# Narrowing weights with ScalarE's sign, two wider products in den_i and a shorter product of ones

## The chip, the cores and the metric

The kernel runs on one core of a Trainium2 chip. The metric is device time in microseconds, from launch to end, as the median of several runs. A core has five engines that run side by side and wait for each other through semaphores: TensorE (PE in the profile; PEld is its loading of weights), VectorE (DVE), ScalarE (ACT), GpSimd (POOL) and SyncE (SP), whose queue issues most of the DMAs.

## The reference

Two blocks follow each other. The first is a linear attention with sketched features, over 4 batches, 4 heads and 1088 positions of 32 numbers:

```python
def phi(x):
    a = np.einsum('rd,bhsd->bhsr', S1, x)
    b = np.einsum('rd,bhsd->bhsr', S2, x)
    return np.einsum('bhsi,bhsj->bhsij', a, b).reshape(*x.shape[:-1], r * r)   # r = 8
q_p, k_p = (phi(q), phi(k))
kv = np.einsum('bhsf,bhsd->bhfd', k_p, v)
z = np.sum(k_p, axis=2)
num = np.einsum('bhsf,bhfd->bhsd', q_p, kv)
den = np.einsum('bhsf,bhf->bhs', q_p, z)[..., None] + 1e-06
attn = (num / den).astype(np.float32)
```

The second takes the result as x with 4352 rows and 128 columns, and is a gated feed-forward layer with 1536 inner columns:

```python
gate = 1.0 / (1.0 + np.exp(-(x @ w_gate)))
val = x @ w_val
out = (gate * val @ w_out).astype(np.float32)
```

S1, S2 and the three weight matrices are given in double precision, q, k and v in single precision. The kernel reads the doubles as pairs of 32-bit words and makes single-precision numbers of them on the chip. This is what "narrowing" means below.

## The kernel before

**Tiling.** The inner dimension of the layer is cut into NJ = 12 blocks of 128, and the tokens into eight chunks of 512 and a last one of 256. A *wave* is one block of one chunk: two products give gate and value (`wave`, L501), ACT makes the sigmoid (`sg`, L509), DVE multiplies (`g`, L540), and a further product adds into the output (`moeout`, L382, in the first chunk; `prod`, L338, in most of the others, which use a scheme with fewer products whose sums POOL forms at L324 and L328). A list `todo` holds the output products back by some waves. Between the waves, `slot` places the steps of the attention of the next batch at wave numbers that are written out by hand.

**Engines' order.** The order of the instructions on PE, DVE, ACT and POOL is the order of the program. SP's order is left to the scheduler.

**The head.** Before the first wave can start, the first half of batch 0 goes through the whole attention: S1 and S2 are narrowed and turned (`st`, L1103), then k is turned (L599), multiplied with S (`kps`, L630), turned back (`kab`, L640), its outer products are formed (`kp`, L709), and from these come `kvz` (L836), its copy `kvd` (L871), the transposed `nd` (L905, L922), the numerators `nps` (L1039) and at last `xT` (L1060), numerators times reciprocals of the denominators. `warm` issues products of ones that nobody reads. One of 256 columns stands right after `st` (L1111), ahead of `kps`; others stand at L1149 and L1171. `den_i` (L989) belongs to the batches 1 to 3: it sums the denominators over the index i, in four products of 32 columns, one for each head, each into its own 32 partitions.

**Narrowing, old form** (`narrow`, L83). A double's high word carries sign, exponent and the upper part of the mantissa; its low word gives three more bits. Six instructions follow each other for each part:

- POOL caps the high word between -122880 and 122880 (`cap`, L97), and ACT makes an integer of the top of the low word (`tail`, L101);
- DVE shifts the capped word left by three and masks it (L105), and puts the sign bit back (L109, `head`);
- ACT squares the capped word (L117), which serves to set small values to zero, and POOL adds `tail` to `head` (L118);
- DVE multiplies `head` by 0 or 1, as the square is under or over a bound, and writes `w_sb` (L127).

The weights are narrowed in parts: part 0 is block 0 of w_gate and w_val, part 1 is block 1 of these, part 2 is blocks 0 and 1 of w_out (`narrow_01`, three parts of 256 columns), and block 2 of all three (`narrow_w(2)`, 384 columns) is the fourth. The first two parts are needed by the first two waves, the third by the first `moeout`, the fourth by the third wave. The blocks 3 to 11 are narrowed in `w1`, between the waves of the first chunk, and are not changed.

Of the kernel before, what the change touches and what calls it, by code (L numbers as in the profile page):

```python
# [20 lines left out]
def kernel(  # L21
# [12 lines left out]
    nc = tc.nc  # L34

    B, H, S, D = q.shape
# [4 lines left out]
    NJ = DFF // P  # L41
# [38 lines left out]
    wide = S1.dtype == I64  # L80
    assert all((a.dtype == I64) == wide for a in (S2, moe_w_gate, moe_w_val, moe_w_out))

    def narrow(out, bits, eng, bank=None, copies=None):  # L83

        p, n, m = bits.shape[:3]
        lo, hi = bits[:, :, :, 0].bitcast(U32), bits[:, :, :, 1]

        def tmp(dt, tag, bufs):
            return sbN.tile([P, 3, P], dt, tag=tag, name=tag, bufs=bufs)[:p, :n, :m]

        cap, tail = tmp(I32, "cap", 6), tmp(I32, "tail", 5)
        eng.tensor_scalar(  # L97
            out=cap.bitcast(F32), in0=hi.bitcast(F32), scalar1=122880.0, scalar2=-122880.0,
            op0=ALU.min, op1=ALU.max,
        )  # L100
        nc.scalar.activation(out=tail, in_=lo, func=ACTF.Copy, scale=2.0**-29)  # L101
        yield

        head = tmp(I32, "head", 3)
        nc.vector.tensor_scalar(  # L105
            out=head, in0=cap, scalar1=3, scalar2=0x3FFFFFF8,
            op0=ALU.logical_shift_left, op1=ALU.bitwise_and,
        )
        nc.vector.scalar_tensor_tensor(  # L109
            out=head, in0=cap, scalar=-0x40000000, in1=head, op0=ALU.bitwise_and, op1=ALU.bitwise_or  # L110
        )
        yield
        square = cap.bitcast(F32)
        if bank:
            square = pso.tile([P, 512], F32, tag=bank, name="square")[:, : n * m]
            square = square.rearrange("p (n m) -> p n m", n=n)
        nc.scalar.activation(out=square, in_=cap.bitcast(F32), func=ACTF.Square)  # L117
        nc.gpsimd.tensor_tensor(out=head, in0=head, in1=tail, op=ALU.add)  # L118
        yield

        head = head.bitcast(F32)
        if copies:
            square, head = (
                bass.AP(tensor=x.tensor, offset=x.offset, ap=[list(x.ap[0]), [0, copies], [1, m]])
                for x in (square, head)
            )
        nc.vector.scalar_tensor_tensor(  # L127
            out=out, in0=square, scalar=1.265625 * 2.0**-30, in1=head, op0=ALU.is_ge, op1=MUL
        )
        yield  # L130


    s4 = const.tile([2 * R, 4, D], F32, tag="s4", name="s4")
# [14 lines left out]
    w_in = {}  # L148
# [40 lines left out]
    def narrow_01(part, step):  # L189
        if wide:  # L190
            if step == 0:
                i = (slice(0, 2), part) if part < 2 else (2, slice(0, 2))
                narrowing["01", part] = narrow(
                    w_sb[:, i[0], i[1]],
                    w_in[0][:, i[0], i[1]],
                    nc.gpsimd,
                    "acc0" if part else "acc1",
                )
            next(narrowing["01", part])


    def load_rows(src, b, t, parts=((0, T, nc.sync),)):
        for t0, t1, eng in parts:
# [95 lines left out]
    )  # L299
    eps = const.tile([P, 1], F32, tag="eps")  # L300
    nc.gpsimd.memset(eps, 1e-6)
    zb = const.tile([P, H, 32], F32, tag="zb", name="zb")
    nc.gpsimd.memset(zb, 0.0)
    nc.gpsimd.memset(v_sb[64:, :, 0], 0.0)
# [181 lines left out]
    def w1():  # L486

        ci = moe["ci"]
        t0, tw = tok_chk[ci]
        jn = TCH // tw  # L490
        j0 = moe["w"] * jn
        wv = psm.tile([P, 2, TCH], F32, tag="wave", name="wave")

        tp = tw // 2 if ci == 0 and j0 == 0 else tw
        turn = (moe["w"] // 2) % 2
        for o in range(0, tw, tp):
            for which in range(2):
                for jj in range(jn):
                    for c in (0,) if ci == 0 else (1 - turn, turn):
                        d = slice(0, P) if ci == 0 else slice(64 * c, 64 * c + 64)  # L500
                        nc.tensor.matmul(  # L501
                            out=wv[d, which, jj * tw + o : jj * tw + o + tp],
                            lhsT=w_sb[:, which, j0 + jj, d],
                            rhs=xT[:, t0 + o : t0 + o + tp],
                            start=True,
                            stop=True,
                        )
        sg = sbG.tile([P, TCH], F32, tag="sg", name="sg")
        nc.scalar.activation(out=sg, in_=wv[:, 0], func=ACTF.Sigmoid)  # L509
        if ci == 0:  # L510
            if j0 == 1:
                narrow_01(2, 3)
            if 0 < j0 < NJ - 2:
                narrow_w(j0 + 1, 3)
            narrow_w(j0 + 2, 1)
            narrow_w(j0 + 2, 2)
            if j0 < 3:
                narrow_w(j0 + 3, 0)
            if j0 > 1:
                narrow_w(j0 + 4, 0)  # L520
            if j0 == NJ - 3:
                weight_sums(0, NJ // 4)
        if ci == 1 and j0 == 1:
            weight_sums(NJ // 4, NJ // 2)
        if moe["w"] % 2 == 0:
            moe["g"] = sbG.tile([P, 2, TCH], F32, tag="g", name="g")
        pair, odd, n = moe["g"], moe["w"] % 2, moe["n"]

        def glu():
            g = pair[:, odd]  # L530
            todo = moe["todo"]
            if jn == 2:
                nc.vector.tensor_tensor(  # L533
                    out=g.rearrange("p (j u s y) -> p j y u s", j=2, u=2, y=4),
                    in0=wv[:, 1].rearrange("p (j y u s) -> p j y u s", j=2, u=2, y=4),
                    in1=sg.rearrange("p (j y u s) -> p j y u s", j=2, u=2, y=4),
                    op=MUL,
                )
            else:
                nc.vector.tensor_tensor(out=g, in0=wv[:, 1], in1=sg, op=MUL)  # L540
            if not fast(ci):
                lag = 4 if ci else 2
                part = (ci, j0, jn, g.rearrange("p (j t) -> p j t", j=jn))
# [443 lines left out]


    def den_i(b, dps):  # L989
        for h in range(H):  # L990
            nc.tensor.matmul(
                out=dps[32 * h : 32 * h + 32],
                lhsT=mask["head"][:, h % 2, :],
                rhs=PD[b][:, h // 2, :],
                start=True,
                stop=True,
            )
        return dps
# [109 lines left out]
        start=True,  # L1108
        stop=True,
    )  # L1110
    warm(256)  # L1111
    st_ = st_[:, : 2 * R].rearrange("p (n r) -> p n r", n=2)
    sk = const.tile([P, 2, 2, R], F32, tag="sk")
    nc.vector.tensor_tensor(
# [28 lines left out]
    mult10 = ab(None, (0, 1, 0), (psm, "wave"))  # L1143
    for pi in range(2):
        outer(0, pi, NJK - 1, NJK, eng=nc.gpsimd)
    for part in range(2):
        narrow_01(part, 0)
    spread_z()
    warm(512)  # L1149
    for pi in range(2):  # L1150
# [6 lines left out]
    def rest(turn, rc, dT):  # L1157
        kv0([1, 2, 3, 4, 0])
        for pi in range(2):
            outer(0, pi, 5, NJK - 1)  # L1160
        kv0(range(5, NJK))
        turn()
        nt = rc.shape[1] - 1
        nc.scalar.activation(out=rc[:, :nt], in_=dT[:, :nt, :2], func=ACTF.Identity, bias=eps)
        kvd(0)
        narrow_01(0, 1)
        narrow_01(0, 2)
        ndt(0)

    divide = dn(0, 0, rest)  # L1170
    warm(256)  # L1171

    def head1():
        narrow_01(1, 1)
        narrow_01(0, 3)
        narrow_01(1, 2)
        narrow_01(2, 0)
        narrow_w(2, 0)

    divide((0, 4), (4, 8), between=head1)  # L1180
    narrow_01(1, 3)
    narrow_01(2, 1)
    narrow_01(2, 2)

    slot(None, 1)
    cq = {}
# [172 lines left out]
```

## Time and profile before

| What | us |
|---|---|
| median of three runs (lowest, highest) | 293.69 (293.63, 294.33) |
| the profiled execution, its own time | 294.1 |
| span of the profiled execution, first to last instruction | 292.3 |
| PE busy | 286.5 |
| DVE busy | 188.8 |
| POOL busy | 162.7 |
| ACT busy | 92.1 |
| first wave starts | 15.28 |
| first moeout starts | 19.33 |

In a line of a timeline the numbers are start and duration in microseconds; then come the engine, the line of the kernel, the operation, what it writes and reads, the shapes, and how many instructions are merged in the line. In brackets stands the idle time of the engine before it, and what ended that. A single-precision product appears as two records, one for each of its two passes. The ends of PE's records are modelled, and successive products overlap in them. The releaser of a wait is inferred, and it is the one that came last by the profile.

### The profile page before, as it was taken

To read this page: it belongs to the slowest core of one execution; us is meant where nothing else is said; L and a number is where in the kernel's file an instruction comes from. 1 tells how busy PE (TensorE), PEld (TensorE's weight loads), DVE (VectorE), ACT (ScalarE), POOL (GpSimd) and SP (SyncE) were. 2 spreads that over 40 slices of the span, in tenths; PEclk is the share of its full clock that TensorE was granted. 3 is DMA by queue.
4 is the path that set the end of the run, shared out by engine and by line. 5 is a ranking of instruction groups with operands and counts; after the bars stand their busy time and mean duration, and the time that the engine had idled before them with its cause. 6 is when DMAs were issued, how large, how long until landed. Compare 5 with 4: busy or idle time off the path is not lost.

```text
span 292.3 us, 5784 instructions
## 1 busy us (share of the span) xinstructions
PE 286.5 (98%) x2276; PEld 154.9 (53%) x2276; DVE 188.8 (65%) x320; ACT 92.1 (32%) x168; POOL 162.7 (56%) x221
## 2 busy tenths in 40 slices
PE   8899999999999999999999999999999999999995
PEld 4444433345455455554555555554555555555895
DVE  6998789985837866677556685668336423642482
ACT  3557542322323222323233213423233222322421
POOL 2365644896646558546446597664465555656300
PEclk9999999999999999999999999999999999999999
DMA  7994522374720187506000584202000200010002
GB/s 216 336 354 87 147 70 84 109 185 111 239 33 0 30 195 148 147 7 183 8 0 2 153 151 108 36 2 37 0 2 0 36 2 0 0 30 8 2 2 54
DMA packets 28890, 24.23 MB, mean 83 GB/s; under 512 B 18560, under 2 KB 24064, under 8 KB 28864
## 3 DMA queue, kind: packets, MB, share of 16 engines
q1 hardware_dynamic: 25808, 21.95, 29.6%
q10 hardware_dynamic: 3056, 1.92, 2.3%
q8 instruction: 18, 0.29, 0.4%
q14 instruction: 8, 0.07, 0.1%
HBM read 20.60 MB, written 3.26 MB: 82 GB/s over the span
## 4 chain that ended last, share of the span: by engine, by line
PE 85%; DMA 6%; DVE 3%; POOL 2%; SPq 1%; issue 1%; ACT 0%; POOLq 0%; ACTq 0%
PE wave L501 55%; PE prod L338 22%; DMA v<-in_v_dram 3%; POOL head L118 2%; DMA w_in<-in_moe_w_out_dram 2%; PE moeout L408 2%; PE moeout L382 1%; PE kvz L849 1%; DVE w_sb L127 1%; DVE head L109 1%; DMA kq<-in_k_dram 1%; PE nps L1214 1%; SPq L157 1%; DVE head L105 1%; PE kps L630 1%
## 5 line engine op out<-in xcount | busy, mean ns | idle before, releaser
L501 PE MATMUL wave<-xT,w_sb 128*64 128x512 f32 (+3 forms) x820 | 210.6, 566 | 0.1
L501 PEld LDWEIGHTS wave<-xT,w_sb 128*64 128x64 f32 (+1 forms) x820 | 85.2, 140 | 63.4 <-issue 49.5
L540 DVE TENSOR_TENSOR g<-wave,sg 128x512 f32<-128x512 f32 x96 | 65.9, 686 | 77.3 <-ACT sg L509 76.2
L509 ACT ACTIVATE sg<-wave 128x512 f32<-128x512 f32 x102 | 61.0, 598 | 170.5 <-PE wave L501 161.0
L328 POOL TENSOR_TENSOR tsum<-g 128x256 f32<-128x256 f32 x84 | 68.1, 813 | 25.6 <-DVE g L540 25.2
L328 POOL TENSOR_TENSOR tsum<-g,tsum 128x256 f32<-128x256 f32 x42 | 35.2, 839 | 59.5 <-DVE g L540 59.2
L338 PE MATMUL prod<-tsum,ws 128*64 128x256 f32 x252 | 62.8, 381 | 0.0
L338 PEld LDWEIGHTS prod<-tsum,ws 128*64 128x64 f32 x252 | 31.2, 136 | 16.8 <-issue 12.4
L338 PE MATMUL prod<-g,w_sb 128*64 128x256 f32 x168 | 34.9, 383 | 0.0
L328 POOL TENSOR_TENSOR tsum<-tsum,g 128x256 f32<-128x256 f32 x42 | 32.9, 782 | 3.3
L338 PEld LDWEIGHTS prod<-g,w_sb 128*64 128x64 f32 x168 | 15.7, 136 | 18.2 <-issue 15.4
L338 PE MATMUL prod<-tsum,w_sb 128*64 128x256 f32 x84 | 25.3, 383 | 0.0
L338 PE MATMUL prod<-g,ws 128*64 128x256 f32 x84 | 25.0, 379 | 0.0
L118 POOL TENSOR_TENSOR head<-head,tail 128x384 int32<-128x384 int32 (+2 forms) x14 | 13.3, 953 | 17.9 <-DVE head L109 11.5
L338 PEld LDWEIGHTS prod<-g,ws 128*64 128x64 f32 x84 | 11.5, 137 | 3.7
L382 PE MATMUL moeout<-g,w_sb 128*128 128x512 f32 (+1 forms) x28 | 12.6, 607 | 0.3 <-DVE w_sb L127 0.3
L338 PEld LDWEIGHTS prod<-tsum,w_sb 128*64 128x64 f32 x84 | 10.8, 137 | 2.4 <-issue 1.9
L709 DVE TENSOR_TENSOR kp<-kab 128x1152 f32<-128x1152 f32 (+2 forms) x10 | 10.9, 1103 | 0.0
L829 DVE TENSOR_TENSOR qp<-qp,bq 128x1152 f32<-128x1152 f32 (+1 forms) x7 | 9.5, 1353 | 1.9 <-DMA a<-dq 1.1
L533 DVE TENSOR_TENSOR g<-wave,sg 128x512 f32<-128x512 f32 x6 | 6.8, 1138 | 4.5 <-ACT sg L509 4.5
L440 DVE TENSOR_TENSOR res<-prod,other 64x512 f32<-64x512 f32 (+1 forms) x14 | 7.6, 544 | 3.0 <-ACT other L434 3.0
L475 DVE STREAM_TRANSPOSE o_sb<-res 64x512 f32<-64x512 f32 x14 | 9.6, 690 | 0.0
(121 smaller groups left out, 203.0 us busy)
## 6 DMA issues: line engine op xcount, KB each, us to landing
qp<-dq SPq DMA_DIRECT2D x7, 576.0 KB
bq<-dq SPq DMA_DIRECT2D x14, 288.0 KB
kq<-in_k_dram SPq DMA_DIRECT2D x3, 544.0 KB
kq<-in_q_dram SPq DMA_DIRECT2D x3, 544.0 KB
w_in<-in_moe_w_out_dram SPq DMA_DIRECT2D x6, 256.0 KB
w_in<-in_moe_w_gate_dram SPq DMA_DIRECT2D x5, 256.0 KB
w_in<-in_moe_w_val_dram SPq DMA_DIRECT2D x5, 256.0 KB
v<-in_v_dram SPq DMA_DIRECT2D x8, 144.0 KB
```

Of the source, the lines that this page charges most:

```text
L118: nc.gpsimd.tensor_tensor(out=head, in0=head, in1=tail, op=ALU.add)
L328: nc.gpsimd.tensor_tensor(out=t[:, u], in0=in0, in1=in1, op=ALU.subtract)
L338: nc.tensor.matmul(out=out, lhsT=lhsT, rhs=rhs, start=start, stop=stop, skip_group_check=True)
L382: nc.tensor.matmul(out=moe["acc"][d], lhsT=w_sb[:, 2, j, d], rhs=g[:, jj], start=(j == 0), stop=(j == NJ - 1),)
L440: nc.vector.tensor_tensor(out=out, in0=in0, in1=in1, op=op)
L475: nc.vector.transpose(out=o_sb[:64, d].rearrange("p t x -> p (t x)"), in_=r[:, 1 + 2 * d : 3 + 2 * d].rearrange("p u x -> p (u x)"),)
L501: nc.tensor.matmul(out=wv[d, which, jj * tw + o : jj * tw + o + tp], lhsT=w_sb[:, which, j0 + jj, d], rhs=xT[:, t0 + o : t0 + o + tp], sta ...
L509: nc.scalar.activation(out=sg, in_=wv[:, 0], func=ACTF.Sigmoid)
L533: nc.vector.tensor_tensor(out=g.rearrange("p (j u s y) -> p j y u s", j=2, u=2, y=4), in0=wv[:, 1].rearrange("p (j y u s) -> p j y u s", j ...
L540: nc.vector.tensor_tensor(out=g, in0=wv[:, 1], in1=sg, op=MUL)
L709: eng.tensor_tensor(out=KP[b][:, pi, j0:j1].rearrange("p j m (i l) -> p (j m) i l", i=R), in0=bass.AP(tensor=a0.tensor, offset=a0.offset, ...
L829: nc.vector.tensor_tensor(out=q0, in0=q0, in1=half(BQ[b], n), op=MUL)
```

## The change

For the first four parts the narrowing is a new class, `Short`, with a method for each step. ACT takes the absolute value of the high word (`bounds`), POOL bounds it from below and above (minimum with 122880 and maximum with a small power of two), ACT turns the low word into a number between 2 and slightly more than 2, whose bits then hold the top of the low word and a constant (`lower`, with a bias tile `two`). DVE shifts by three (`shift`, one instruction in place of two), POOL adds (`total`), ACT takes the sign of the high word into a bank of PSUM (`sign`), and DVE multiplies head by sign (`final`). So DVE issues two instructions for a part instead of three, ACT three instead of two, and POOL two as before. `narrow` stays for S1 and S2 and for the blocks 3 to 11, and does the same as before.

The steps also stand at other places: the last multiplication of part 2 is issued behind the sigmoid of the first wave, ahead of the first `g`, where the old order had it behind that `g`; that of the fourth part comes right after it.

In `den_i`, two products of 64 columns, one for each pair of heads, take the place of four of 32. The product of ones after `st` has 64 columns instead of 256. A memset for the bias tile is new.

```diff
+    class Short:
+        def __init__(self, out, bits):
+            tmp, self.lo, self.hi = pieces(bits)
+            self.out = out
+            self.cap, self.tail = tmp(F32, "cap", 6), tmp(F32, "tail", 5)
+            self.head = tmp(I32, "head", 3)
+        def bounds(self):
+            nc.scalar.activation(out=self.cap, in_=self.hi.bitcast(F32), func=ACTF.Abs)
+            nc.gpsimd.tensor_scalar(
+                out=self.head.bitcast(F32), in0=self.cap, scalar1=122880.0, scalar2=2.0**-15,
+                op0=ALU.min, op1=ALU.max,
+            )
+        def lower(self):
+            nc.scalar.activation(
+                out=self.tail, in_=self.lo, func=ACTF.Identity, bias=two, scale=2.0**-51
+            )
+        def shift(self):
+            nc.vector.tensor_scalar(
+                out=self.head, in0=self.head, scalar1=3, scalar2=None, op0=ALU.logical_shift_left
+            )
+        def total(self):
+            nc.gpsimd.tensor_tensor(
+                out=self.head, in0=self.head, in1=self.tail.bitcast(I32), op=ALU.add
+            )
+        def sign(self, bank):
+            self.sgn = bank_of(self.cap, bank)
+            nc.scalar.activation(out=self.sgn, in_=self.hi.bitcast(F32), func=ACTF.Sign)
+        def final(self):
+            nc.vector.tensor_tensor(
+                out=self.out, in0=self.sgn, in1=self.head.bitcast(F32), op=MUL
+            )
...
+    short = []
+    def step(name, *parts, **how):
+        for n in parts if wide else ():
+            if n == len(short):
+                i = ((slice(0, 2), 0), (slice(0, 2), 1), (2, slice(0, 2)), (slice(0, 3), 2))[n]
+                jj = i[1] if n < 3 else 0
+                short.append(Short(w_sb[:, i[0], i[1]], w_in[n // 3][:, i[0], jj]))
+            getattr(short[n], name)(**how)
...
+    two = const.tile([P, 1], F32, tag="two_", name="two_")
+    nc.gpsimd.memset(two, 2.0)
...
         if ci == 0:
+            if j0 == 0:
+                step("final", 2)
+                step("sign", 3, bank="acc1")
             if j0 == 1:
-                narrow_01(2, 3)
-            if 0 < j0 < NJ - 2:
+                step("final", 3)
+            if 1 < j0 < NJ - 2:
                 narrow_w(j0 + 1, 3)
-            narrow_w(j0 + 2, 1)
-            narrow_w(j0 + 2, 2)
+            if j0 > 0:
+                narrow_w(j0 + 2, 1)
+                narrow_w(j0 + 2, 2)
...
     def den_i(b, dps):
-        for h in range(H):
+        for pi in range(2):
             nc.tensor.matmul(
-                out=dps[32 * h : 32 * h + 32],
-                lhsT=mask["head"][:, h % 2, :],
-                rhs=PD[b][:, h // 2, :],
+                out=dps[64 * pi : 64 * pi + 64],
+                lhsT=mask["head"].rearrange("p m x -> p (m x)"),
+                rhs=PD[b][:, pi, :],
...
-    warm(256)
+    warm(64)
...
-    for part in range(2):
-        narrow_01(part, 0)
+    step("bounds", 0, 1)
+    step("lower", 0, 1)
...
         kvd(0)
-        narrow_01(0, 1)
-        narrow_01(0, 2)
+        step("shift", 0, 1)
+        step("total", 0, 1)
+        step("sign", 0, bank="acc1")
         ndt(0)
...
     def head1():
-        narrow_01(1, 1)
-        narrow_01(0, 3)
-        narrow_01(1, 2)
-        narrow_01(2, 0)
-        narrow_w(2, 0)
+        step("final", 0)
+        step("sign", 1, bank="acc0")
+        step("bounds", 2, 3)
+        step("lower", 2, 3)
     divide((0, 4), (4, 8), between=head1)
-    narrow_01(1, 3)
-    narrow_01(2, 1)
-    narrow_01(2, 2)
+    step("final", 1)
+    step("shift", 2, 3)
+    step("total", 2, 3)
+    step("sign", 2, bank="acc1")
```

More of the change, by code (lines that the diff above doesn't have):

```diff
@@ L81, with pieces, bank_of, narrow @@
     assert all((a.dtype == I64) == wide for a in (S2, moe_w_gate, moe_w_val, moe_w_out))
-    def narrow(out, bits, eng, bank=None, copies=None):
+    def pieces(bits):
         p, n, m = bits.shape[:3]
-        lo, hi = bits[:, :, :, 0].bitcast(U32), bits[:, :, :, 1]
         def tmp(dt, tag, bufs):
             return sbN.tile([P, 3, P], dt, tag=tag, name=tag, bufs=bufs)[:p, :n, :m]
+        return tmp, bits[:, :, :, 0].bitcast(U32), bits[:, :, :, 1]
+    def bank_of(x, bank):
+        p, n, m = x.shape
+        t = pso.tile([P, 512], F32, tag=bank, name="square")[:p, : n * m]
+        return t.rearrange("p (n m) -> p n m", n=n)
+    def narrow(out, bits, eng, bank=None, copies=None):
+        tmp, lo, hi = pieces(bits)
         cap, tail = tmp(I32, "cap", 6), tmp(I32, "tail", 5)
@@ L112, in narrow @@
         yield
[L113 to L116, printed above, removed]
+        square = bank_of(cap, bank) if bank else cap.bitcast(F32)
         nc.scalar.activation(out=square, in_=cap.bitcast(F32), func=ACTF.Square)
@@ L123, in narrow @@
             square, head = (
-                bass.AP(tensor=x.tensor, offset=x.offset, ap=[list(x.ap[0]), [0, copies], [1, m]])
+                bass.AP(tensor=x.tensor, offset=x.offset, ap=[list(x.ap[0]), [0, copies], list(x.ap[2])])
                 for x in (square, head)
@@ L186, in narrow_w @@
             next(narrowing[j])
[L189 to L199, printed above, removed]
+    short = []
[6 more added lines that the diff above has]
+            getattr(short[n], name)(**how)
     def load_rows(src, b, t, parts=((0, T, nc.sync),)):
```

## The prediction

> **What bounds the kernel now.** I read the page's busy time first, then the busy time by stage, then each engine's timeline in the stage that the diff touches.
>
> ```profile
> PE 286.5 (98%) x2276; PEld 154.9 (53%) x2276; DVE 188.8 (65%) x320; ACT 92.1 (32%) x168; POOL 162.7 (56%) x221
> 11.00:15.30 4.30, 3.29 (x100) 1.95 (x100) 4.20 (x13) 2.32 (x7) 1.39 (x3) 1.00 1.03 364
> 15.30:20.30 5.00, 4.66 (x15) 2.59 (x16) 4.62 (x11) 2.55 (x6) 3.24 (x6) 1.00 1.06 372
> 20.30:41.00 20.70, 20.70 (x55) 8.59 (x54) 16.80 (x33) 11.93 (x24) 12.06 (x16) 1.00 0.44 105
> 57.00:292.30 235.30, 232.07 (x1909) 131.77 (x1904) 140.58 (x219) 66.31 (x113) 133.31 (x171) 1.00 0.26 61
> ```
>
> The stage lines give stretch, length, then busy time of PE, PEld, DVE, ACT and POOL, the clock and the DMA. From 20.3 us on PE never stops, and its timeline shows one idle gap there, 0.24 us at 41.09. So work taken from another engine after 20 us is worth nothing; only PE's own work and the start of the waves count. In the head (5.5 to 20.3 us) it is the other way round: DVE is busy 4.20 of 4.30 and 4.62 of 5.00 us, and PE waits. That is where the narrowing of the first four parts lies.
>
> DVE's timeline, before the first wave (start, duration, engine, line, operation):
>
> ```profile
> 12.37 0.25 DVE L105 TENSOR_SCALAR head<-cap 128x256 int32<-128x256 int32 x1
> 12.65 0.43 DVE L109 SCALAR_TENSOR_TENSOR head<-cap,head 128x256 int32<-128x256 int32 x1
> 12.99 0.25 DVE L1055 RECIPROCAL rc<-rc 128x16 f32<-128x16 f32 x1
> ...
> 14.13 0.42 DVE L109 SCALAR_TENSOR_TENSOR head<-cap,head 128x256 int32<-128x256 int32 x1
> 14.48 0.42 DVE L127 SCALAR_TENSOR_TENSOR w_sb<-square,head 128x256 f32<-128x256 f32 x1
> 14.81 0.41 DVE L1060 TENSOR_TENSOR xT<-nps,rb 128x256 f32<-128x256 f32 x1
> ```
>
> and PE's in the same stretch:
>
> ```profile
> 13.92 0.67 PE L1039 MATMUL nps<-qp,nd 64*32 64x256 f32 x16 [0.35 <-ACT nd L922]
> 14.51 0.70 PE L260 MATMUL warm<-const-float32-1.0 128*128 128x256 f32 x2
> 15.28 3.71 PE L501 MATMUL wave<-xT,w_sb 128*128 128x256 f32 x12
> 19.33 1.12 PE L382 MATMUL moeout<-g,w_sb 128*128 128x512 f32 x2 [0.34 <-DVE w_sb L127]
> 20.29 1.88 PE L501 MATMUL wave<-xT,w_sb 128*128 128x512 f32 x4
> ```
>
> The first wave starts at 15.28, just after xT (14.81 + 0.41 = 15.22), the last of a DVE queue without a gap. The first moeout waits for w_sb of part 2.
>
> **What the Trainium skill says.** "ScalarE: Activation LUTs", section "What ACT_TABLE_LOAD costs": an activation with immediate scale and bias takes 186 + 0.833 ns per column, a bias tile adds 93 ns, and a table load takes 1283 ns, with the drain 2.66 us. The trace agrees: 0.39 us at 256 columns (the formula gives 0.40), one load of 1.28 us. The same page, "Table sets: the hidden batching unit": cheap functions (relu, copy, identity, abs are named) are in every set. Sign is not named there; no run here shows Abs or Sign yet. "TensorE: Matmul & The Clock Gate", "The HAM clock gate": half rate until PE has been busy for a window of some 3.4 us. The trace agrees on the rates: the opening 512-column records start 0.855 us apart (1.76, 2.61, 3.47, 4.32), the same width later 0.43. "TensorEngine Tiling (Array Packing)", "Key Properties": a change of tiling mode drains the array; used for den_i below.
>
> **The change, part by part.**
>
> *Shorter product of ones (256 to 64 columns, after st).*
>
> ```profile
> 5.52 0.99 PE L260 MATMUL warm<-const-float32-1.0 128*128 128x256 f32 x2
> 6.44 0.18 PEld L630 LDWEIGHTS kps<-kT,sk 64*32 64x32 f32 x16 [0.42 <-DVE qT L610]
> ```
>
> At half rate two passes of 256 columns stream 2 x 0.43 us: 5.52 + 0.85 = 6.37, and kps follows at 6.44. The releaser column names qT, which ends at 5.74 + 0.70 = 6.44. But a released start comes 0.05 us after its releaser elsewhere (zb ends at 11.15, dps loads at 11.20), and here 0.00, so I take the product of ones as the cause. With 64 columns the streams are 2 x 0.11; the two weight loads (0.50 us in all) then set most of it, about 0.55 to the drained end: kps near 6.10. Gain **0.35**; ends: 0 if qT is the real wait, 0.57 if only sk (5.64 + 0.18 + 0.05 = 5.87) holds kps. DVE idles 0.76 us before kab for kps, and qT is done at 6.44, so the gain passes on: from kab (7.20) DVE runs without a gap to the kvz chain. The weights of parts 0 and 1 land at an unmoved time (the first L101 at 10.07 waits for a DMA), 2 us before they are needed.
>
> *Narrowing of the four parts.* L105 and L109 become one shift: each part loses an L109, 0.43 us at 256 columns. Ahead of xT two go: 12.65 to 12.99 and 14.13 to 14.48, 0.69 us of DVE's queue. But xT also needs nps, which ends at 13.92 + 0.67 = 14.59. So xT goes from 14.81 to about 14.63, gain **0.18**, and late next is kvz, kvd, ndps, nd, nps, in which nothing changes.
>
> Behind it the L109 of part 2 (16.60 to 16.94) and of weight block 2 (17.33 to 18.26) go as well, and the last multiplication of part 2 moves ahead of g. Without the common shift: final 1 is done at about 15.8, both shifts at 16.4, POOL's add of part 2 (0.73) at 17.2, final 2 at 17.65. sg waits for the whole first wave, 17.31 - 0.18 = 17.13, then 0.60 and g 0.68: 18.45. PE is through its second wave at 15.10 + 3.71 - 0.16 = 18.65 (successive products overlap by 0.16: 23.68 + 1.88 against a start at 25.40). So moeout starts at 18.65, with no wait. Gain there 0.34 + 0.16 = **0.50**, and 0.08 more since the next wave (20.29) no longer trails its own start-up. That wave needs final 3: POOL's second add (1.00) ends at 18.2, DVE finishes at 18.95; it is due at 19.5. Ends 0.3 and 0.6.
>
> *ScalarE* gets three activations for two: 3 x 0.39 + 0.49 = 1.7 us, and 4 x 0.09 for the bias tile. The cover: it idles 1.71 us until rc at 12.54, and four activations from 10.07 end at 11.75. After nd six activations, 2.7 us with their overlap, run from 13.5 to about 16.2, and sg is due at 16.8 to 17.1. The sign of block 2 reuses the bank acc1 and waits for final 2; queued behind it are L101 of block 3 and the second sg, which needs the second wave (18.8) anyway. Price 0, end 0.6 late. POOL's minimum/maximum stays one instruction, the added memset (0.10, as eps) lies in idle time. No DMA is added or moved.
>
> *The gap at 41.09.* DVE gains some 1.1 us by block 2 (its w_sb was started at 19.55, now 18.4), PE 0.76 without the common shift, so the last qmult ends earlier against PE. Half of the 0.24 is a change of tiling and stays: **0.12**, ends 0 and 0.12.
>
> *den_i.* Three times, each so:
>
> ```profile
> 75.91 0.48 PE L991 MATMUL nps<-pd,head 128*32 128x160 f32 x8
> 76.31 0.65 PE L338 MATMUL prod<-g,w_sb 128*64 128x256 f32 x4
> ```
>
> The four products run side by side: two passes of 160 columns stream 2 x 0.43 x 160/512 = 0.27 us, yet the step to prod is 0.41. Two products of 64 columns stream as long, so nothing is halved. But they have prod's own tiling (128\*64), so the drain between (0.41 - 0.27 = 0.14, part of it the first product's start-up) and prod's slower first pass (0.27, its second passes begin at 76.58; later ones follow every 0.215: 76.80, 77.01) go, 0.16 each; 3 x 0.16 = **0.48**, ends 0 and 0.5. PE has no slack there, so it counts in full.
>
> Sum: 0.35 + 0.18 + 0.58 + 0.12 + 0.48 = **1.7 us**. The profiled execution took 294.1 us (span 292.3 and 1.8 around it): 292.4. It lies 0.4 above the median of the three runs (293.69), so against the median I forecast **292.0**.
>
> **Rivals.**
> (1) *Only part arrives.* kps really waits for qT, and den_i's drain merely moves to its front. Then 0.18 + 0.58 + 0.12 = 0.9 us: 292.8. For it: the releaser column, and that numerators (64\*32) stand ahead of den_i, so one drain stays in any case. Against: the 0.00 us, and waves and prods of one tiling that follow without a gap.
> (2) *The change lengthens the cold time*: less work of ones, the rise to full rate one window later. kps, aps and bps would take 0.45 each more, of which DVE's 0.76 us of idle time hides part: gain 0.7, 293.0. For it: the head's full rate begins only after 5.5. Against: PE is idle for just 0.1 us more.
> (3) *Slower: Sign is missing from sigmoid's table set.* Each switch is 2.66 us by the page. Place: Sign before nd on the path to xT (one), then back for sg, Sign, back for sg: four, of which some 2 us are hidden: +8.6 - 1.7, 300.6. A single unhidden switch already outweighs the gain, so it decides from the first load on. For it: the page doesn't name Sign. Against: Copy, Square, Identity and Sigmoid share one load, and the change uses no costly function.
>
> **Numbers.** Forecast 0.64, (1) 0.20, (2) 0.09, (3) 0.07. What a measurement can tell from no change is 0.3%, 0.9 us. Case (1) lies on that bound and is split: faster 0.64 + 0.09 = 0.73, same 0.19, slower 0.08. Range: the upper ends (0.57 + 0.18 + 0.6 + 0.12 + 0.5 = 2.0) and the runs' spread of 0.4 give 291.3; (1) and (2) with their spread give 293.4.
>
> **What would show it.** Right: kps near 6.1, xT right after nps, first wave near 14.75, moeout with no wait near 18.3, later events about 1.2 us earlier, and 1.7 after the third den_i, with prod 0.27 us behind den_i. Wrong: kps still at 6.44, a second table load on ACT, sg or w_sb as releaser of a PE wait of over 0.3 us before 25 us, or a new PE gap after 41 us.

## Result: 0.46% faster

| | before | after |
|---|---|---|
| median of 22 runs each, us | 294.19 | 292.87 |
| lowest, highest | 293.61, 295.29 | 292.20, 296.02 |
| ratio after/before, 95% interval | | 0.9954 (0.9939 to 0.9969) |

By the ratio, 1.35 us were gained (0.9 to 1.8) where 1.7 was forecast. The absolute time is 0.87 above the forecast of 292.0. Of these, 0.50 come from before itself, whose median over 22 runs is that much higher than the one over three runs that I started from; the other 0.37 is gain that did not arrive.

The profile after is of one execution, and it happens to be the slowest of the 22: 296.02 us, span 294.1. By the clock records of its trace, which give the rate granted to TensorE, it ran at half rate until 13.6 us. The busy times on its page hardly tell the change:

```profile
PE 288.8 (98%) x2264; PEld 156.6 (53%) x2264; DVE 186.5 (63%) x316; ACT 93.7 (32%) x172; POOL 160.6 (55%) x222
```

DVE has 4 instructions fewer, PE 12 (three den_i, two products fewer in each, two passes a product), ACT 4 more, as the diff says. TensorE's timeline shows the half rate:

```profile
6.30 1.21 PE L673 MATMUL kps<-kT,sk 64*32 64x288 f32 x16
7.44 1.16 PE L780 MATMUL aps<-qT,s 32*64 32x256 f32 x16
11.29 2.06 PE L297 MATMUL warm<-const-float32-1.0 128*128 128x512 f32 x2
17.37 3.71 PE L540 MATMUL wave<-xT,w_sb 128*128 128x256 f32 x12
20.92 1.02 PE L421 MATMUL moeout<-g,w_sb 128*128 128x512 f32 x2
```

kps took 0.72 us before and takes 1.21 here, aps 0.69 and 1.16. The first wave starts 2.09 us later than before, although its work is shorter. From there on the gain shows even here: the first moeout starts 3.55 us after the wave (4.05 before) and waits for nothing. Two signs can be read in spite of the rate. VectorE's timeline and ScalarE's table load:

```profile
5.97 0.14 DVE L1157 TENSOR_TENSOR sk<-st,hm 128x32 f32<-128x32 f32 x1
6.04 0.68 DVE L653 STREAM_TRANSPOSE qT<-kq 128x512 f32<-128x512 f32 x1
```

```profile
L300 ACT ACT_TABLE_LOAD  x1: 1283/1283/1283, 1.7 to 1.7; - x1
```

qT ends at 6.72, and kps started at 6.30: kps does not wait for qT. And Abs and Sign cost no second table load.

The same kernel, run again (label e4_again below), gave a profile at full rate: span 291.3, own time 293.07. It is the one to compare with the profile before. Its busy times by stage, in the columns used above:

```profile
11.00:15.30 4.30, 3.56 (x102) 2.27 (x95) 3.52 (x11) 2.68 (x8) 1.92 (x4) 1.00 1.06 371
15.30:20.30 5.00, 5.00 (x16) 2.77 (x15) 4.29 (x11) 4.14 (x9) 3.25 (x5) 1.00 1.06 372
57.00:291.30 234.30, 230.73 (x1888) 132.02 (x1884) 138.60 (x217) 65.90 (x113) 130.85 (x170) 1.00 0.26 60
```

DVE is no longer full before the first wave (3.52 of 4.30 us, 4.20 before), and PE never stops between 15.3 and 20.3 (5.00, was 4.66). In the last stretch it idles a little more (234.30 - 230.73 = 3.57 us, before 235.30 - 232.07 = 3.23). Of this, 3.2 us lie behind the last products, at the end of the program, in both; the new 0.31 lies near 74 us and is the subject of the experiments. PE's timeline of it:

```profile
6.03 0.72 PE L673 MATMUL kps<-kT,sk 64*32 64x288 f32 x16
13.51 0.67 PE L1082 MATMUL nps<-qp,nd 64*32 64x256 f32 x16 [0.35 <-ACT nd L965]
14.76 3.71 PE L540 MATMUL wave<-xT,w_sb 128*128 128x256 f32 x12
18.30 1.02 PE L421 MATMUL moeout<-g,w_sb 128*128 128x512 f32 x2
19.16 1.88 PE L540 MATMUL wave<-xT,w_sb 128*128 128x512 f32 x4
```

and DVE's:

```profile
13.18 0.42 DVE L168 TENSOR_TENSOR w_sb<-square,head 128x256 f32<-128x256 f32 x1
14.28 0.42 DVE L1103 TENSOR_TENSOR xT<-nps,rb 128x256 f32<-128x256 f32 x1 [0.67 <-PE nps L1082]
16.95 0.42 DVE L168 TENSOR_TENSOR w_sb<-square,head 128x256 f32<-128x256 f32 x1 [0.64 <-POOL head L159]
17.42 0.69 DVE L583 TENSOR_TENSOR g<-wave,sg 128x512 f32<-128x512 f32 x1
```

xT now waits for nps (idle 0.67 in front of it) where it stood at the end of a full queue. The first wave is at 14.76, the first moeout at 18.30 without a wait, and part 2's `w_sb` is written ahead of `g`.

To follow the gain down the program I compare the starts of the same sigmoid in two traces: the first (0), the third (2), the thirteenth (12, after the gap at 41 us), the 23rd (22, after the first den_i) and the 101st (100, after all three). Microseconds against the profile before, minus is earlier:

| kernel | 0 | 2 | 12 | 22 | 100 |
|---|---|---|---|---|---|
| after, the profile at half rate | +2.09 | +1.48 | +1.26 | +2.11 | +1.83 |
| after again (e4) | -0.52 | -1.13 | -1.35 | -0.75 | -1.03 |
| narrowing alone (e3) | -0.16 | -0.76 | -0.98 | -0.98 | -0.98 |
| ones alone (e1) | -0.43 | -0.43 | -0.45 | +0.13 | +0.13 |
| den_i alone (e2) | -0.25 | -0.25 | -0.28 | -0.41 | -0.69 |

The first column also carries what differs in the head between executions: e2 changes nothing there and is 0.25 early. So differences of 0.2 to 0.3 at sigmoid 0 prove nothing by themselves; the steps between columns don't have this doubt.

In the row of e4, 1.35 us have arrived by sigmoid 12. Then 0.60 is lost again before sigmoid 22, although den_i gives about 0.14 there. Most of the experiments are about that loss.

### The profile page after: what moved, and what is told of

It reads as the page before. It is cut to its first block, busy times and chain, and to the rows that moved or that the text cites. A ratio compares the mean times of both kernels' runs of the same rounds, so it can differ in the third digit from the quotient of the medians.

```text
span 294.1 us, 5762 instructions
## 1 busy us (share of the span) xinstructions
PE 288.8 (98%) x2264; PEld 156.6 (53%) x2264; DVE 186.5 (63%) x316; ACT 93.7 (32%) x172; POOL 160.6 (55%) x222
## 3 DMA queue, kind: packets, MB, share of 16 engines
q10 hardware_dynamic: 3056, 1.92, 2.3%
## 4 chain that ended last, share of the span: by engine, by line
PE 89%; DMA 7%; SPq 1%; DVE 0%; issue 0%; ACT 0%; DVEq 0%
PE wave L540 55%; PE prod L377 20%; DMA bq<-dq 5%; PE moeout L421 4%; PE moeout L447 2%; PE warm L297 1%; PE kps L673 1%; SPq L844 1%; PE nps L1258 1%; DMA s_in<-in_S_dram 1%; PE kvz L892 1%; PE cqps L819 1%; DMA dq<-cq 1%; DMA b<-dq 1%; PE denj L1021 0%; PE dps L1063 0%
## 5 line engine op out<-in xcount | busy, mean ns | idle before, releaser
L367 POOL TENSOR_TENSOR tsum<-g,tsum 128x256 f32<-128x256 f32 x42 | 34.2, 814 | 57.8 <-DVE g L583 57.6
L117 POOL TENSOR_TENSOR head<-head,tail 128x384 int32<-128x384 int32 (+1 forms) x10 | 9.9, 987 | 13.9 <-DVE head L111 12.6
```

Of the source, the lines that this page charges most:

```text
L367: nc.gpsimd.tensor_tensor(out=t[:, u], in0=in0, in1=in1, op=ALU.subtract)
```

## Experiments

Letters in the expectations name theories. In short: A is the prediction's sum, each term arriving at the end of the program in full; the later letters put the missing part down to the transfers of batch 1's features, or ask what splits the executions; F says that the ones are worth little once TensorE has its full rate; G, the last, asks which half of the narrowing step carries its gain.

### The three parts by themselves, and the whole again

e1: before, with only

```diff
-    warm(256)
+    warm(64)
```

> The kernel before with the product of ones after st cut from 256 to 64 columns, nothing else. Theory A (the product of ones held kps, and its end passes on): kps starts within 0.25 us of the end of sk, 0.3 to 0.5 us earlier against sk than before, and the time falls by about 0.35 us. Theory B (kps waits for the turned q): kps starts 0.05 us after the end of the turned q, time unchanged. Theory C (the shorter product lets TensorE's half rate last longer in part of the executions): the runs spread more widely than those of before, some of them 1 to 3 us longer, and the median is level or higher.

e2: before, with only den_i's two products of 64 columns (the hunk of den_i in the diff above).

> The kernel before with den_i in two products of 64 columns, nothing else. Theory A (a change of tiling falls away behind den_i): the first prod starts about 0.27 us behind den_i instead of 0.41, three times, and the time falls by 0.4 to 0.5 us. Theory B (the drain merely moves ahead of den_i): den_i starts 0.1 us later behind the numerators, time unchanged within 0.15 us.

e3: after, with `warm(256)` and den_i's four products put back, so narrowing alone.

> The changed kernel with den_i in four products and 256 columns of ones as before: the new narrowing alone. Theory A (DVE's shorter queue): xT starts within 0.1 us of the end of nps, the first moeout starts without a wait, the sigmoids from the third on are 0.75 us earlier against the first input's arrival, the time falls by 0.75 to 0.9 us. Theory B (ScalarE or GpSimd becomes late instead): a PE wait on w_sb or g before 25 us of over 0.3 us, and the time falls by less than 0.4 us.

e4: after, unchanged.

> The changed kernel once more, for a second profile. Theory A (the half rate up to 13.6 us in the first profile was one execution's own): the rise to full rate comes before 8 us, kps starts about 0.2 us after sk, the first wave starts near 14.75 us, the span is near 290.7 us. Theory C (the shorter product of ones regularly delays the rise): the half rate lasts past 9 us again, and the first wave starts after 15.5. On the wait of denj for a DMA (1.0 us in the first profile): if it belongs to the change, it is there again with over 0.5 us; if it is the DMAs' own spread, it can be absent.

| | median (lowest, highest), runs | ratio to before | us |
|---|---|---|---|
| e1 ones | 294.10 (293.64, 294.27), 14 | 0.9997 (0.9989 to 1.0005) | -0.09 |
| e2 den_i | 293.67 (293.33, 295.12), 14 | 0.9990 (0.9979 to 1.0002) | -0.29 |
| e3 narrowing | 293.52 (292.84, 294.53), 14 | 0.9979 (0.9967 to 0.9990) | -0.62 |
| e4 all | 292.66 (292.21, 293.12), 6 | 0.9952 (0.9937 to 0.9967) | -1.41 |

The last column is (ratio - 1) times 294.16, the median of before measured beside these four. Every table below has its own runs of before beside it, and the ratio is to those. The parts sum to -1.0, within the interval of the whole.

**Narrowing** carries most of it: 0.16 at the first wave, 0.60 more by the third sigmoid, 0.22 more at the gap at 41 us. **den_i** does in the trace what its step says, three times 0.14. PE's timeline of e2, to be held against 75.91 and 76.31 before:

```profile
75.63 0.49 PE L991 MATMUL nps<-pd,head 128*64 128x160 f32 x4
75.95 0.60 PE L338 MATMUL prod<-g,w_sb 128*64 128x256 f32 x4
76.38 0.38 PE L338 MATMUL prod<-g,ws 128*64 128x256 f32 x1
```

From den_i to prod it is 0.32 (0.40 before), from prod to the next product 0.43 (0.49 before, 76.31 to 76.80). In time its interval still touches no change.

**The ones.** PE's lines of e1, then DVE's:

```profile
5.47 0.43 PE L260 MATMUL warm<-const-float32-1.0 128*128 128x64 f32 x2
6.01 0.72 PE L630 MATMUL kps<-kT,sk 64*32 64x288 f32 x16
```

```profile
5.82 0.14 DVE L1114 TENSOR_TENSOR sk<-st,hm 128x32 f32<-128x32 f32 x1
```

kps starts 0.05 us after sk's end at 5.96, and the first wave is 0.43 earlier than before. In the profile before, kps started 0.63 after sk's end:

```profile
5.64 0.18 DVE L1114 TENSOR_TENSOR sk<-st,hm 128x32 f32<-128x32 f32 x1
```

Only a small part of that difference can be put down to the shorter product. The two executions also differ in TensorE's rate: by the clock records the full rate began at 5.0 us in e1's and at 6.15 in the one before. In e3, with 256 columns and full rate from 5.3 us on, kps follows sk by 0.14:

```profile
5.48 0.70 PE L297 MATMUL warm<-const-float32-1.0 128*128 128x256 f32 x2
6.11 0.71 PE L673 MATMUL kps<-kT,sk 64*32 64x288 f32 x16
5.83 0.14 DVE L1157 TENSOR_TENSOR sk<-st,hm 128x32 f32<-128x32 f32 x1
```

All 14 profiled executions fit the same pattern (times in us; e5 to e12 are described below):

| columns of ones | full rate from | kps after sk's end | profiles |
|---|---|---|---|
| 256 | 6.15, 6.20 | 0.63, 0.61 | before, e9 |
| 256 | 5.86 | 0.36 | e5 |
| 256 | 3.6 to 5.3 | 0.14 | e2, e3, e8 |
| 64 | 6.10, 13.58 | 0.32, 0.19 | e10, after |
| 64 | 4.0 to 5.3 | 0.05 to 0.07 | e1, e4, e6, e7, e11, e12 |

So the shorter product brings kps 0.3 to 0.4 us forward where the half rate still holds at that time, and about 0.08 where it doesn't. The median of e1, -0.09 us, is what the second case would give.

In the one execution of e1 that was profiled, even the early start was lost again, between sigmoids 12 and 22. PE's timeline of e1 there, and the last line of VectorE's before it:

```profile
74.08 0.92 PE L978 MATMUL denj<-b,zw 64*32 64x160 f32 x16
74.95 1.15 PE L1214 MATMUL nps<-qp,nd 64*32 64x512 f32 x32
74.22 0.68 DVE L540 TENSOR_TENSOR g<-wave,sg 128x512 f32<-128x512 f32 x1
```

From denj to the numerators (`nps`) it takes 0.87 us. Before it took 0.29, 0.58 less:

```profile
74.53 0.50 PE L978 MATMUL denj<-b,zw 64*32 64x160 f32 x16
74.82 1.16 PE L1214 MATMUL nps<-qp,nd 64*32 64x512 f32 x32
```

In e4 a releaser stands beside denj's second half (the last line is VectorE's again):

```profile
73.17 0.48 PE L1021 MATMUL denj<-b,zw 64*32 64x160 f32 x8
73.96 0.48 PE L1021 MATMUL denj<-b,zw 64*32 64x160 f32 x8 [0.31 <-DMA b<-dq]
74.19 1.16 PE L1258 MATMUL nps<-qp,nd 64*32 64x512 f32 x32
73.46 0.68 DVE L583 TENSOR_TENSOR g<-wave,sg 128x512 f32<-128x512 f32 x1
```

1.02 in place of 0.29: a loss of 0.73. It closes the row of e4: -1.35 - 0.14 + 0.73 = -0.76, for the -0.75 there. `denj` multiplies the tile b of batch 1, and a multiplication on VectorE behind it reads the tile a. Both are spread over the partitions by DMAs from memory, and in e4 half of b had not landed.

Something else held the numerators at least as long. Their tile has the tag of the waves' tiles (`wave`, L1225 of the kernel before), so I infer that it takes over a bank that a `g` must have read first. The times agree: `g` ends at 74.22 + 0.68 = 74.90 in e1 and the numerators start at 74.95; in e4 the two are 74.14 and 74.19, in the first profile of after 77.00 and 77.06. And `g` stands in VectorE's queue behind the multiplication of qp by bq, which reads what the same transfers bring. Nothing waited on PE there before, but this multiplication already did. Its line in the profile before:

```profile
72.32 1.74 DVE L829 TENSOR_TENSOR qp<-qp,bq 128x1152 f32<-128x1152 f32 x1 [1.15 <-DMA a<-dq]
```

It ends at 74.06 and `g` behind it at 74.66, 0.16 before the numerators' start at 74.82. So in that execution an earlier PE would have met transfers with almost nothing to spare. In e1 the multiplication starts at 72.79, 0.47 later than before, and in e4 at 72.18, hardly earlier, though everything ahead of it had come earlier. In e3 it started at 70.10 without waiting, denj took its 0.30, and the 0.98 went through. The transfers differ that much between executions.

### Making the spread's b transfers larger

If four transfers of b, 32 partitions each, are merged into two of 64, b might land earlier. In each of the four kernels (before; ones of 64; after; after with ones of 256):

```diff
         for x in range(2):
+            d0 = d[2, 0]
+            put.dma_start(
+                out=B8[b][64 * x : 64 * x + 64],
+                in_=bass.AP(
+                    tensor=d0.tensor,
+                    offset=d0.offset + W1 * x,
+                    ap=[[2 * W1, 2], [8 * W1, 32], [1, W1]],
+                ),
+            )
             for m in range(2):
                 p0 = 64 * x + 32 * m
-                for i, t in enumerate((A8[b], B8[b])):
...
+                d0 = d[m, 0]
+                put.dma_start(
+                    out=A8[b][p0 : p0 + 32],
...
```

The order of issue changes with it: each half's b now goes ahead of its two transfers of a, where a and b took turns.

> The kernel before with the b part of each spread in two DMAs of 64 partitions instead of four of 32, so six small DMAs stand behind the large ones and the last need not wait for the last large one. Theory D (denj of batch 1 waits for these DMAs in some executions, before the change too): no execution waits there, the last b lands 2 us earlier, and the time falls by 0.2 to 0.5 us. Theory E (the wait is rare before the change): time unchanged within 0.15 us.

> The same with 64 columns of ones after st. Theory D (the wait of denj took what the shorter product of ones gained): no wait at denj, 0.3 to 0.5 us under the same kernel with 256 columns. Theory F (the product of ones costs little once TensorE has full rate, so it was never worth 0.35 us): under 0.2 us of difference.

> The changed kernel with the b part in two DMAs of 64 partitions. Theory D: no wait at denj, 0.3 to 0.7 us under the changed kernel, and 1.5 to 1.8 us under the kernel before with the same DMAs. Theory E: as the changed kernel within 0.15 us.

> The changed kernel with the b part in two DMAs and 256 columns of ones again. Theory A (the shorter product is worth 0.35 us): 0.3 us or more slower than with 64 columns. Theory F: within 0.2 us of it. Theory C (the shorter product makes long half rates likelier): fewer executions over 1 us above the median than with 64 columns.

| | median (lowest, highest), runs | ratio to before |
|---|---|---|
| e5 before, b merged | 295.76 (294.87, 300.69), 18 | 1.0060 (1.0037 to 1.0082) |
| e6 ones 64, b merged | 296.70 (294.30, 298.91), 12 | 1.0072 (1.0040 to 1.0104) |
| e7 after, b merged | 295.37 (292.71, 299.14), 19 | 1.0014 (0.9995 to 1.0033) |
| e8 after, ones 256, b merged | 295.05 (293.56, 300.18), 22 | 1.0027 (1.0005 to 1.0050) |

A miss: by their medians e5, e6 and e7 are slower than the same kernels without it (e8's was not run without it). The last b lands later, not earlier, as PE's timeline of e7 shows:

```profile
73.37 0.48 PE L1029 MATMUL denj<-b,zw 64*32 64x160 f32 x8
75.31 0.34 PE L1029 MATMUL denj<-b,zw 64*32 64x160 f32 x4 [1.47 <-DMA b<-dq]
```

1.94 us between the two halves of denj, against 0.79 in e4. In e5 the numerators come 1.83 after denj (74.42, 76.25), 1.54 more than before, and its median is 1.4 us (295.76 over 294.33) above before. So what is late here does cost time. The pairs e5 and e6, e7 and e8 were to show what the ones are worth with b out of the way. b wasn't out of the way, the runs spread over 4 to 7 us (those of before beside them over 4.7, from 293.45 to 298.18), and nothing on the ones follows from these medians. Larger transfers and their new order were not tried apart.

### Taking denj's wait away

Here denj of batch 1 reads ones in place of b, and the multiplication behind it ones in place of a; the DMAs are still issued. The right denominators of batch 1 are left out. The multiplication of qp by bq still waits for its transfers. In before, in ones of 64, and in after:

```diff
-                    rhs=B8[b][rows, (W1 - WD) * (x // 2) : (W1 - WD) * (x // 2) + WD],
+                    rhs=nc.const_aps.tensor(1.0, [P, WD], F32)[rows] if b == 1 else B8[b][rows, (W1 - WD) * (x // 2) : (W1 - WD) * (x // 2) + WD],
...
-        nc.vector.tensor_tensor(out=PD[b], in0=t[:, :, :WD], in1=A8[b], op=MUL)
+        ones = nc.const_aps.tensor(1.0, [P, 2, WD], F32)
+        nc.vector.tensor_tensor(
+            out=PD[b], in0=t[:, :, :WD], in1=ones if b == 1 else A8[b], op=MUL
+        )
```

> The kernel before, in which denj of batch 1 reads ones instead of what the a and b DMAs of that batch bring (so the denominators of batch 1 are left out; the DMAs are still issued). Theory D (denj's wait for these DMAs is what splits the executions into two groups 0.6 us apart and takes gains of the head): no execution in the upper group, the median 0.3 to 0.6 us under the kernel before. Theory E (the wait is rare and the groups come from the clock): median unchanged within 0.15 us.

> The same with 64 columns of ones after st. Theory D: now the shorter product shows, 0.2 to 0.5 us under the same kernel with 256 columns. Theory F (it is worth little because TensorE has full rate by then in most executions): under 0.15 us of difference.

> The changed kernel in which denj of batch 1 reads ones in the same way. Theory D: 1.6 to 1.9 us under the kernel before with the same edit, so the forecast 1.7 comes back once the wait is away. Theory E: 1.3 to 1.4 us, as measured with the wait.

| | median (lowest, highest), runs | ratio to before |
|---|---|---|
| e9 before, freed | 294.20 (293.51, 295.58), 14 | 0.9999 (0.9983 to 1.0015) |
| e10 ones 64, freed | 294.45 (293.96, 298.86), 14 | 1.0016 (0.9993 to 1.0038) |
| e11 after, freed | 293.07 (292.04, 295.61), 11 | 0.9966 (0.9944 to 0.9988) |

In e9 freeing denj gains the kernel before nothing that can be measured (-0.5 to +0.4 us); the profile before had shown no wait there either. e10 was to let the ones' gain through, and did not: its median lies 0.25 above that of e9. DVE's timeline of e10, then PE's:

```profile
72.79 1.65 DVE L829 TENSOR_TENSOR qp<-qp,bq 128x1152 f32<-128x1152 f32 x1 [1.92 <-DMA a<-dq]
```

```profile
74.22 0.50 PE L978 MATMUL denj<-const-float32-1.0,zw 64*32 64x160 f32 x16
75.09 1.15 PE L1217 MATMUL nps<-qp,nd 64*32 64x512 f32 x32 [0.37 <-DVE g L540]
```

denj no longer waits, but the numerators behind it do: they come 0.87 us after denj, as in e1. The releaser column names g; what had made VectorE late is the line above, qp waiting 1.92 us for a DMA. So the transfers hold the program at two places, and opening one leaves the other. The gain of 0.31 at sigmoid 12 became a loss of 0.28 at sigmoid 22. No run took the wait of qp away.

In e11's profile the transfers happened to be early. DVE's line, then PE's:

```profile
69.86 1.36 DVE L872 TENSOR_TENSOR qp<-qp,bq 128x1152 f32<-128x1152 f32 x1
```

```profile
73.25 0.51 PE L1021 MATMUL denj<-const-float32-1.0,zw 64*32 64x160 f32 x16
73.55 1.16 PE L1261 MATMUL nps<-qp,nd 64*32 64x512 f32 x32
```

0.30 between them, no wait, and sigmoid 100 comes 1.68 earlier than before; that execution took 292.51 (before's 294.1). The 1.7 of the forecast is there in this one execution, with the luck of early transfers. The median of e11 lies 1.3 below that of before, 1.0 by the ratio, and 1.1 below that of e9. That is no better than after's own gain and misses the 1.6 to 1.9 of theory D, so the freed tiles alone gain nothing over the runs.

### Where part 2's last multiplication and the fourth sign stand

e12: after, with the two steps behind the first `g` again.

```diff
         if ci == 0:
-            if j0 == 0:
+            if j0 == 1:
                 step("final", 2)
                 step("sign", 3, bank="acc1")
-            if j0 == 1:
                 step("final", 3)
```

> The changed kernel with the last multiplication of part 2 and the sign of the fourth part put back behind the first g, as the kernel before had them. Theory A (the L109s that fell away end the wait of the first moeout by themselves): moeout waits for less than 0.1 us, time as the changed kernel within 0.15 us. Theory G (the new place of the multiplication does it): w_sb of part 2 is written 0.7 us later than with the new place, at about 18.1 to 18.6 us, moeout starts 0.3 us later and the third wave waits for the fourth part; the time is 0.3 to 0.6 us longer.

Measured: 293.87 (293.39 to 295.23, 14 runs), ratio 0.9995 (0.9980 to 1.0009): the gain is gone. That is 1.0 us above after's median (1.2 by the ratios), more than the 0.3 to 0.6 expected. DVE's timeline of e12:

```profile
17.10 0.69 DVE L582 TENSOR_TENSOR g<-wave,sg 128x512 f32<-128x512 f32 x1 [1.00 <-ACT sg L548]
17.70 0.41 DVE L168 TENSOR_TENSOR w_sb<-square,head 128x256 f32<-128x256 f32 x1
19.29 0.56 DVE L168 TENSOR_TENSOR w_sb<-square,head 128x384 f32<-128x384 f32 x1 [1.17 <-ACT square L165]
```

and ScalarE's and PE's behind it:

```profile
18.68 0.51 ACT L165 ACTIVATE square<-w_in 128x384 f32<-128x384 f32 x1
```

```profile
14.44 3.71 PE L540 MATMUL wave<-xT,w_sb 128*128 128x256 f32 x12
18.17 1.13 PE L421 MATMUL moeout<-g,w_sb 128*128 128x512 f32 x2
19.90 1.98 PE L540 MATMUL wave<-xT,w_sb 128*128 128x512 f32 x4 [0.61 <-DVE w_sb L168]
```

The fourth part's sign needs the bank that part 2's multiplication frees. Behind the first `g` that is at 17.70 + 0.41, and the sign stands in ScalarE's queue behind the second sigmoid, at 18.68 (17.41 in e4). VectorE idles 1.17 us for it, and PE 0.61 before the third wave. Between sigmoids 0 and 2 e12 loses 0.56 against before, and e4 gains 0.61, with the same instructions on every engine.

The first moeout changes little. It starts 3.73 us after the first wave in e12, 3.54 in e4, 4.05 before: the L109s that fell away bring 0.32 of this by themselves, the new place 0.19. The large difference is the third wave, which starts 1.73 us after the first moeout in e12, 0.86 in e4, 0.96 before. The two steps were moved together, not one by one.

## Why the prediction was right, and where it was not

- **Bound.** Right: before 20 us VectorE's queue set the start of the waves. PE's own work after 20 us did count (den_i below). That an earlier start of the waves reaches the end in full, because PE's timeline has one gap only, doesn't hold in every execution (see the sum).
- **xT earlier, 0.18.** 0.16 in e3, within what the head varies. Counted from the start of nps, xT comes 0.77 later in e3 and e4 and 0.89 before, so 0.12 is the change's own. xT follows nps with VectorE idle in front, as it should. kvz, kvd, ndps, nd, nps were late next, as named.
- **First moeout's wait, 0.50 + 0.08.** 0.60 (e3) and 0.61 (e4) between sigmoids 0 and 2. moeout at 18.30 and without a wait, as forecast. But I named the fallen L109s and the new place together, and priced little beyond moeout's wait. e12 shows that the place matters most for the third wave: with the old one the shorter form loses 0.56 in this stretch. The prediction says that this wave needs final 3, but not what the old place would have cost it.
- **Gap at 41.09, 0.12.** 0.22 by sigmoid 12 (e3, e4), above the upper end I gave. From the wave to dps it is 1.80 in e4 (38.01, 39.81), 1.96 before, so 0.16 of the gap went, where I had put half of the 0.24 down to a change of tiling that stays. The other 0.06 I can't place.
- **ScalarE at nothing.** Right. One table load, and no PE wait for sg or `w_sb` before 25 us. "ScalarE: Activation LUTs", section "What ACT_TABLE_LOAD costs", has a formula from which I estimate 0.40 us for 256 columns and 0.51 for 384; Sign took 0.41 and 0.51 to 0.53, and Abs 0.43 and 0.56, a little more. Rival (3) is out.
- **den_i, 0.48.** 0.41 in the trace (0.13 or 0.14 each, for 0.16). den_i to prod is 0.32, not 0.27. In time it is -0.29, which can't be told from nothing. den_i starts 1.09 us after the numerators in e2 as before (74.54 to 75.63, 74.82 to 75.91), so no drain moved ahead of it.
- **Ones, 0.35.** The term that was mis-sized: in time it is -0.09 (-0.32 to +0.15). The step that failed is taking the half rate at 5.5 us, seen in one execution, for the kernel's usual state. In three of the six profiles with 256 columns the full rate came earlier, kps followed sk by 0.14, and 0.08 was left to gain. Where the half rate does last, the price was right (0.63 or 0.61 against 0.32). The first wave at 14.76, where 14.75 was forecast, is luck: kps came closer to sk by 0.58, of which 0.49 goes with the earlier full rate, while sk itself ended 0.16 later.
- **The sum.** In e4 the steps of the table come to 0.52 + 0.61 + 0.22 + 0.41 = 1.76, for the forecast's 1.71. The wait at the transfers takes 0.73, and 1.03 is left: 294.1 - 1.03 = 293.07, that execution's time. But the 0.52 contains the earlier full rate. An estimate from the traces at equal rate is 0.12 + 0.08 + 0.60 + 0.22 + 0.41 = 1.43, and the ratios give 1.35 and 1.41. So the measured gain needs no loss at the transfers; the small worth of the ones is enough. That such a loss occurs is shown in single executions, and what it costs over many is not: freeing denj changed nothing measurable, and the wait of qp was not taken away. The premise that failed there is that no gap on PE means that nothing else is due. VectorE's wait for a DMA at 72.32 stood in the profile before, and the prediction has no term for it.
- **Rival (1)**, only part arrives. The gain of 1.35 lies about midway between its 0.9 and the forecast's 1.7, but its mechanism is out: kps starts before qT is done (6.01 against 6.57 in e1), with 256 columns too (6.11 against 6.84 in e3), and den_i's drain did not move to its front.
- **Rival (2)**, a longer half rate, did occur: in the profiled execution of after, 3 us dear and the only one of the 22 above 293.6. In the seven other profiles with the shorter product (e1, e4, e6, e7, e10, e11, e12) the full rate began by 6.1 us. That the shorter product caused the one late rise is not shown. "TensorE: Matmul & The Clock Gate", section "The HAM clock gate", asks for a busy window of about 3.4 us. The trace of that execution doesn't agree: PE was busy for 4.64 of the 4.80 us from 0.7 to 5.5, and for all of 5.5 to 13.6, and kept the half rate to the end of that. A rise to full rate at a fixed time after work begins can't be counted on here.

**Open.** The runs of before fall into two groups, around 293.7 and 294.6, and those of after around 292.3 and 292.9. The runs of e9 still spread over both, which speaks against denj's wait as the cause; what it is stays open. Nor is it settled whether the parts help each other (-1.0 as a sum, -1.4 together; the intervals overlap). Narrowing and den_i with the longer product of ones was not run alone.

## What to carry to other kernels

A profile is one execution. A saving priced at the rate or the wait that it happens to show may be worth little in the others: find a second profile in which that state differs. Before counting a gain in full, look further down for the transfers and other engines that are just in time, also where the bounding engine shows no gap; an engine off the path that already waits for a DMA marks a place where it can be lost. When a short chain is split over two engines' queues, its place in each queue can be worth more than the instructions saved. A wait taken away shows what is late next: price that before removing it.

## What was not expected of the hardware

- The full rate of TensorE began between 3.6 and 6.2 us in the clock records of 13 of the 14 profiled executions, and at 13.6 in one; that one took 3.2 us more than the median of its kernel (296.02, 292.87). Even between 3.6 and 6.2 the moment matters: a product of 256 columns issued at about 5.5 us held its follower until 0.14 us after sk or until 0.63.
- In the profiled execution of e6 PE waited for b twice around the first half of denj, for 0.39 and 2.22 us (to 77.09). By the clock records it then ran at half rate from 76.9 to 80.3 us: 28 records of the numerators took 2.04 us, 1.12 in e7, where the longest such wait was 1.47 and the rate stayed full. This is one execution; that the idle time caused the fall was not tested.
- The same transfers of batch 1 let qp start at 69.9 to 70.1 us in two profiles (e3, e11) and at 72.0 to 72.9 in seven others without merging and with full rate from the head on.
- Two DMAs of 64 partitions for four of 32, each issued ahead of a's, made the last data land later: 1.94 us between the halves of denj, for 0.79.
